# Moving the odd heads' keys on SyncE's queue in two parts, with ScalarE's key tiles ordered chunk by chunk

## The chip, the cores and the metric

The kernel runs on one core of one Trainium2 chip. A core has five engines that run side by side and wait for each other through semaphores: TensorE (matrix products), VectorE, ScalarE, GpSimd and SyncE (which here only issues transfers). The metric is the device time of one execution in microseconds. The profile is one further execution, recorded by the hardware profiler.

## What is computed

An attention with 32 heads that share one set of keys and values (head size 16, 2048 rows, width 512), and a gated MLP over the same rows, are mixed by a sigmoid gate.

```python
x = A_x                                             # 2048 x 512, bf16
g = sigmoid((x * gate_w).sum(-1, keepdims=True))
# A: 32 heads of 16, one key and one value head
q = (x @ wq).reshape(B, S, 32, 16).transpose(0, 2, 1, 3)
k, v = x @ wk, x @ wv
p = softmax(einsum('bhqd,bkd->bhqk', q, k) * 16 ** -0.5)
a = einsum('bhqk,bkd->bhqd', p, v).transpose(0, 2, 1, 3).reshape(B, S, 512) @ wo
# B: gelu, layer norm of one half, product with w_sp over the rows
z = gelu(x @ w_in)
z1, z2 = z[..., :688], layernorm(z[..., 688:])
b = (z1 * (w_sp @ z2 + b_sp)) @ w_out
out = g * a + (1 - g) * b
```

## The kernel before

**The attention in units.** The 2048 queries are cut into four chunks of 512, and the 32 heads into groups of eight. A unit is one query chunk with four heads, of even or of odd number in a group of eight; there are 32 units, even and odd in turn. The keys are cut into 16 tiles of 128 (tile kt belongs to chunk kt // 4). For one unit there are 64 blocks of scores: 16 tiles times four heads. Four heads use four row groups of 32 of TensorE at once.

**Keys for even and odd heads.** `KA` holds the transposed keys twice. `KA[:, 0, :]` has them in rows 0 to 15 of each row group of 32, for the even heads, and comes from VectorE's copy of a product in PSUM, one copy for each chunk (`k_ev`, line 355). `KA[:, 1, :]` has the same keys in rows 16 to 31, for the odd heads. [...]`k_shift` (line 359) issues four of them (one for each row group, all 2048 keys) on GpSimd's queue after chunk 3 has been copied.

**Two ways to an exponential.** ScalarE takes `exp` of two blocks at a time from PSUM into `P` (line 631). VectorE takes other blocks: a batch is one tile with four heads, and it makes a polynomial of the score by a scale and shift of two blocks at a time (`d_A`, line 655) and two squarings (`d_square`, line 667), into `X`; GpSimd can take pieces of 416 columns of the second squaring (line 674). A correction (`MC`, `CC`, made from `Kt` and the values) is added for the tiles that VectorE took in a unit. P and X are then multiplied with the values (`V1`) into one accumulating bank per unit.

**Which tile goes where.** `KL` lists the tiles: ScalarE takes a unit's tiles from its front, VectorE from its end, at most `NMAX` = 7 of them. `Kt` has keys replicated for the tiles that VectorE may take.

**The order is made by a planner.** A simulation in the kernel's Python code holds costs of each piece and due times (`T`), steps through TensorE, ScalarE and VectorE, and writes down each engine's instructions in the order in which it would start them. That order is fixed in the program; each engine follows its own list and waits on semaphores for the data. `T["K1"]` is the time from which the planner lets odd units begin. The first groups on TensorE are values and keys by chunk (`first`), then the correction, then queries, then the MLP's products (`g_z2`, `z1_mm`, `g_sp`).

**Fillers.** The planner counts TensorE's work of the last 3400 ns and puts in products that nobody reads (`ones`, `zeros`, in `keep_pick`) where it is under `KEEP`.

**Transfers.** At the start SyncE's queue issues the transposed loads of x, then the MLP's weights (`win`, `bspz`, `wo`, `wout`), then with `ld_wT(0)` four transposed loads of `w_sp` (line 302), each after the one before has landed. They are first used by `g_sp`.

```python
KL = (0, 1, 2, 4, 5, 8, 9, 12, 13, 6, 10, 14, 15, 11, 7, 3)
q = when(("Q", u // 2), ("K", 0, KL[un["hi"] // 4 - 1] // 4)) if u % 2 == 0 else when(("Q", u // 2), "K1")
rk = [("K", 0, kt // 4)] if par == 0 else [("K", 1, g)]
```

## Time and profile before

| | us |
|---|---|
| runs | 741.61, 739.71, 743.42, 744.69 |
| median of the runs | 742.52 |
| the profiled execution | 746.55 |
| its span | 744.7 |
| TensorE busy | 700.5 (94%) |
| VectorE busy | 713.5 (96%) |
| ScalarE busy | 719.0 (97%) |
| GpSimd busy | 303.2 (41%) |

The span is the time from the first to the last instruction of the profiled execution; 1.85 us of its time lie around it. A line of the profile's list of groups names the line of the code, the engine, the operation, what is written and read with its shape, how often, then the busy time and the mean of one in ns, and the idle time of the engine just before and what ended it. L312 and L313 are the helper that records every matmul, so these are told apart by their operands: `ps<-QA,KA` are scores, `ps<-P,V` and `ps<-X,V` the products with the values, `ps<-xT,wk_rep` keys, `ps<-wvg,xT` values and the gate, `ps<-ones,zeros` fillers. A timeline gives start and length of merged instructions of one kind, and in brackets the idle time before and its releaser.

### The profile page before, as it was taken

What the parts mean: (1) busy time and instruction counts of PE and PEld (TensorE: products, weight loads), DVE (VectorE), ACT (ScalarE), POOL (GpSimd) and SP (SyncE); (2) the same over time, 40 slices, a digit from 0 to 9 for tenths busy, and PEclk for the clock granted to TensorE, in tenths of its full rate; (3) what the DMA queues carried; (4) which work ended last, traced back from release to release, by engine and by line L of the source; (5) the groups of instructions that cost most, each with busy time, mean ns of one, the idle gap of its engine ahead of it and who ended that gap; (6) DMA issues with size and microseconds to landing.
All of it is one profiled execution on the core that took longest, in us unless ns stands there. A gap on an engine that the chain in (4) does not pass through costs nothing.

```text
span 744.7 us, 14117 instructions
## 1 busy us (share of the span) xinstructions
PE 700.5 (94%) x5529; PEld 192.4 (26%) x5529; DVE 713.5 (96%) x821; ACT 719.0 (97%) x781; POOL 303.2 (41%) x304
## 2 busy tenths in 40 slices
PE   8999999999899999999999999999999999999995
PEld 2222222223322223222222322222222222223221
DVE  7789999999999999999999999999999999999996
ACT  5789999999999999999999999999999999999994
POOL 4234334441434544444344343434454333334440
PEclk9779999999999999999999999999999999999998
DMA  9810000000000000600000050000005000000000
GB/s 193 191 34 1 1 1 1 1 1 1 1 1 1 1 1 2 116 13 15 1 1 1 2 121 15 8 1 1 1 2 113 16 15 1 1 1 1 1 1 33
DMA packets 49115, 17.06 MB, mean 23 GB/s; under 512 B 44146, under 2 KB 48978, under 8 KB 49043
## 3 DMA queue, kind: packets, MB, share of 16 engines
q1 hardware_dynamic: 45986, 15.02, 9.4%
q10 hardware_dynamic: 2928, 0.82, 0.6%
q8 instruction: 45, 0.74, 0.4%
q0 software_dynamic: 128, 0.26, 0.2%
q14 instruction: 28, 0.22, 0.1%
HBM read 3.25 MB, written 2.10 MB: 7 GB/s over the span
## 4 chain that ended last, share of the span: by engine, by line
ACT 57%; PE 22%; issue 17%; DVE 3%; DMA 1%; ACTq 0%
ACT P L631 55%; PE ps L313 14%; PE ps L312 7%; DVE X L655 1%; DMA xT<-in_A_x_dram 1%; ACT z L521 1%; DVE X L667 1%; ACT z L529 1%; DVE KA L355 0%; ACTq L161 0%; ACT L631 0%; ACT L529 0%; DVE outsb L1321 0%; DVE T L685 0%; DVE OT L700 0%
## 5 line engine op out<-in xcount | busy, mean ns | idle before, releaser
L631 ACT ACTIVATE P<-ps 128x1024 bf16<-128x1024 f32 x752 | 692.5, 1114 | 8.1 <-PE ps L313 7.8
L313 PE MATMUL ps<-QA,KA 32*128 32x512 bf16 x2048 | 320.2, 388 | 32.8 <-ACT P L631 27.3
L655 DVE TENSOR_SCALAR X<-ps 128x1024 f16<-128x1024 f32 x272 | 329.8, 1213 | 9.1 <-PE ps L313 7.9
L674 POOL TENSOR_TENSOR X<-X 128x416 bf16<-128x416 f16 x189 | 166.2, 879 | 348.8 <-DVE X L667 257.0
L667 DVE TENSOR_TENSOR X<-X 128x2048 f16<-128x2048 f16 (+3 forms) x272 | 291.0, 1076 | 2.0
L313 PEld LDWEIGHTS ps<-QA,KA 32*128 32x128 bf16 x2048 | 78.0, 91 | 322.3 <-ACT P L631 291.0
L313 PE MATMUL ps<-P,V 128*32 128x512 bf16 x1504 | 138.7, 389 | 0.0
L691 POOL TENSOR_TENSOR rc<-T,mone 128x16 f32<-128x16 f32 x31 | 94.7, 3056 | 54.4 <-DVE T L685 54.3
L312 PE MATMUL ps<-wT,z 128*128 128x512 bf16 x320 | 100.3, 385 | 0.0
L313 PE MATMUL ps<-X,V 128*32 128x512 bf16 x544 | 67.0, 388 | 0.2 <-DVE T L685 0.2
L313 PEld LDWEIGHTS ps<-P,V 128*32 128x32 bf16 x1504 | 28.6, 94 | 44.1 <-issue 43.2
L312 PEld LDWEIGHTS ps<-wT,z 128*128 128x128 bf16 x320 | 22.5, 97 | 47.6 <-issue 43.2
L312 PE MATMUL ps<-wout,z 128*128 128x512 bf16 x96 | 29.9, 385 | 0.7 <-DVE sq L613 0.4
L312 PE MATMUL ps<-win,xT 128*128 128x344 bf16 x128 | 29.6, 314 | 0.1
L685 DVE STREAM_TRANSPOSE T<-ps 128x512 f32<-128x512 f32 x32 | 22.7, 710 | 3.4 <-PE ps L313 3.3
L312 PE MATMUL ps<-ones 128*128 128x512 bf16 x64 | 22.3, 426 | 1.5 <-DVE ones L256 1.5
L312 PE MATMUL ps<-wo,OT 128*128 128x512 bf16 x64 | 21.4, 385 | 1.6 <-DVE OT L700 1.6
L697 POOL TENSOR_TENSOR Tn<-T,rcg 128x256 bf16<-128x256 f32 x31 | 21.3, 687 | 2.4
L312 PE MATMUL ps<-xT,wq 128*128 128x512 bf16 x64 | 20.5, 396 | 0.0
L312 PE MATMUL ps<-ones,zeros 128*128 128x512 bf16 x54 | 20.5, 406 | 0.0
L313 PEld LDWEIGHTS ps<-X,V 128*32 128x32 bf16 x544 | 15.6, 94 | 17.8 <-issue 15.7
L312 PE MATMUL ps<-xT,win 128*128 128x512 bf16 x80 | 18.3, 380 | 0.9 <-ACT z L521 0.7
(113 smaller groups left out, 293.6 us busy)
## 6 DMA issues: line engine op xcount, KB each, us to landing
out_dram<-outsb SPq DMA_DIRECT2D x14, 128.0 KB, 1.7
win<-in_B_w_in_dram SPq DMA_DIRECT2D x2, 688.0 KB, 6.0
wout<-in_B_w_out_dram SPq DMA_DIRECT2D x1, 640.0 KB, 9.2
wo<-in_A_wo_dram SPq DMA_DIRECT2D x1, 512.0 KB, 7.1
wq<-in_A_wq_dram ACTq DMA_DIRECT2D x1, 384.0 KB, 8.5
wT<-in_B_w_sp_dram SPq DMA_TRANSPOSE x16, 4.5
KA<-KA POOLq DMA_DIRECT2D x4, 64.0 KB, 3.5
out_dram<-outsb ACTq DMA_DIRECT2D x2, 128.0 KB, 3.3
```

The source lines that it names most:

```text
L312: return t.matmul(dst, lhsT, rhs, start=start, stop=stop)
L313: return t.matmul(dst, lhsT, rhs, start=start, stop=stop, tile_position=tp)
L521: op("act", lambda a: a.activation(z1[:, 1024 * i:1024 * i + 1024], bank(b, 1024), ACT.Gelu_apprx_tanh), r=[bkey(b), bkey(b + 1)], w=[("z1 ...
L529: op("act", lambda a: a.activation(z, z, ACT.Gelu_apprx_tanh), r=[("z2", st) for st in sts], w=[("z2", st) for st in sts], tag="gelu2")
L631: op("act", lambda a: a.activation(P[:, 512 * p:512 * (p + n)], ps[:, 512 * b0:512 * (b0 + n)], ACT.Exp), r=[bkey(b0 + i) for i in range(n ...
L655: op("dve", lambda v: v.tensor_scalar(X[:, m % NX, 1024 * h:1024 * h + 1024], bank(BD, 1024), PA, PB, ALU.mult, ALU.add), r=[bkey(BD), bke ...
L667: op(eng, lambda v: v.tensor_tensor(x if tag == "dU" else x.bitcast(B16), x, x, ALU.mult), r=ks, w=ks, tag=tag)
L674: op("pool", lambda g: g.tensor_tensor(x.bitcast(B16), x, x, ALU.mult), r=ks, w=ks, after=[pg.ops["dve"][-1]], tag="gW")
L685: o("dve", lambda v: v.transpose(T1[:], bank(BO)), r=[("bk", BO)], w=["T1"], tag="T1")
L691: o("pool", lambda g: g.tensor_tensor(rc[:].unsqueeze(2), lsum, mone[:].unsqueeze(2), ALU.pow), r=["T1", "mone"], w=["rc"], tag="rc")
L697: o(e, lambda v: v.tensor_tensor(tn, t1[:, :, 0:16], s_[:].unsqueeze(2).broadcast_to([128, 16, 16]), ALU.mult), r=["T1", k], w=[("Tn", pr, ...
```

## The change

The list of tiles is reordered so that ScalarE's front part has three tiles each of chunks 0, 1 and 2 and then the tiles of chunk 3, and VectorE's end is 3, 7, 11, 15, 14, 13, 12. The keys of the odd heads are moved in two parts, on SyncE's queue: keys 0 to 1535 after chunk 2 is copied, keys 1536 to 2047 after chunk 3 is. The first transposed loads of `w_sp` are issued behind the second part. Score products of odd units wait for the part that they read. The planner's `T["K1"]` is 5000 ns after chunk 3 in place of 4500. `Kt` gets the one tile of each of the chunks 0, 1, 2 and all four of chunk 3 that VectorE may now take.

```diff
-KL = (0, 1, 2, 4, 5, 8, 9, 12, 13, 6, 10, 14, 15, 11, 7, 3)
+KL = (0, 1, 2, 4, 5, 6, 8, 9, 10, 12, 13, 14, 15, 11, 7, 3)
...
-        ld_wT(0)
...
-        def k_shift():
+        def k_shift(z):
+
+            lo, hi = ((0, 1536), (1536, S))[z]
             for g in range(4):
-                dma("pool", lambda q, g=g: q.dma_start(KA[32 * g + 16:32 * g + 32, 1, :], KA[32 * g:32 * g + 16, 0, :]),
-                    r=[("K", 0, c) for c in range(4)] + ["KA1"], w=[("K", 1, g)], tag="Ksh")
+                dma("sp", lambda q, g=g: q.dma_start(KA[32 * g + 16:32 * g + 32, 1, lo:hi], KA[32 * g:32 * g + 16, 0, lo:hi]),
+                    r=[("K", 0, c) for c in (range(3) if z == 0 else (3,))] + ["KA1"], w=[("K", 1, g, z)], tag="Ksh")
...
+                if c == 2:
+                    k_shift(0)
                 if c == 3:
-                    k_shift()
-                    T["K1"] = t + 4500
+                    k_shift(1)
+                    ld_wT(0)
+                    T["K1"] = t + 5000
...
-                dve_q.append((330, lambda: op("dve", lambda v: v.tensor_copy(
-                    Kt[:, 2 * c:2 * c + 2, :].rearrange("p k (h d) -> p k h d", d=DH),
-                    KT0[:, 4 * c + 2:4 * c + 4, :].unsqueeze(2).broadcast_to([128, 2, 8, DH])), r=[("KT0", c)], w=[("Kt", c)], tag="Kt"), t, setT(("Kt", c))))
+                n, k0 = (1, 4 + c) if c < 3 else (4, 0)
+                dve_q.append((66 + 134 * n, lambda: op("dve", lambda v: v.tensor_copy(
+                    Kt[:, k0:k0 + n, :].rearrange("p k (h d) -> p k h d", d=DH),
+                    KT0[:, 4 * c + 4 - n:4 * c + 4, :].unsqueeze(2).broadcast_to([128, n, 8, DH])), r=[("KT0", c)], w=[("Kt", c)], tag="Kt"), t, setT(("Kt", c))))
...
-                        Kt[:, 2 * (kt // 4) + kt % 2, :] if h == 0 else ones[:, 0:128], V1[:, kt, :].unsqueeze(1).broadcast_to([128, NMAX - i, 32]),
+                        Kt[:, kt - 12 if kt > 11 else 4 + kt // 4, :] if h == 0 else ones[:, 0:128], V1[:, kt, :].unsqueeze(1).broadcast_to([128, NMAX - i, 32]),
...
-            rk = [("K", 0, kt // 4)] if par == 0 else [("K", 1, g)]
+            rk = [("K", 0, kt // 4)] if par == 0 else [("K", 1, g, kt // 12)]
```

## The prediction

> **What bounds the kernel now.** I read the page first, then ScalarE's timeline, then TensorE's, then a table of stretches. The page says which engine the end hangs on, and where the TensorE clock was not at full speed.

> ```profile
> span 744.7 us, 14117 instructions
> PEclk9779999999999999999999999999999999999998
> ACT 57%; PE 22%; issue 17%; DVE 3%; DMA 1%; ACTq 0%
> L631 ACT ACTIVATE P<-ps 128x1024 bf16<-128x1024 f32 x752 | 692.5, 1114 | 8.1 <-PE ps L313 7.8
> ```

> ScalarE's 752 exponentials are the longest part of the chain, and in the whole run they idle only 8.1 us. So the kernel is bound by ScalarE, and only those 8.1 us, the 10 us before the first exponential and the 10.7 us after the last are to be had. The second and third of the forty slices (18.6 to 55.9 us) have a granted clock of 0.7. ScalarE's timeline puts nearly all of the idle time there:

> ```profile
> 9.98 13.14 ACT L631 ACTIVATE P<-ps 128x1024 bf16<-128x1024 f32 x14 [0.49 <-PE ps L313]
> 24.56 3.77 ACT L631 ACTIVATE P<-ps 128x1024 bf16<-128x1024 f32 x4 [1.44 <-PE ps L313]
> 28.74 1.02 ACT L631 ACTIVATE P<-ps 128x1024 bf16<-128x1024 f32 x1 [0.31 <-PE ps L313]
> 46.02 1.02 ACT L631 ACTIVATE P<-ps 128x1024 bf16<-128x1024 f32 x1 [0.49 <-PE ps L313]
> 48.50 12.02 ACT L631 ACTIVATE P<-ps 128x1024 bf16<-128x1024 f32 x13 [0.16 <-PE ps L313]
> ```

> Fourteen exponentials run without a gap (0.939 us each), then one wait of 1.44 us, and from 28 to 48 us nearly every one waits for its score matmuls. TensorE's timeline shows what came first:

> ```profile
> 22.54 0.81 PE L312 MATMUL ps<-ones,zeros 128*128 128x512 bf16 x3
> 24.13 0.40 PE L313 MATMUL ps<-QA,KA 32*128 32x512 bf16 x4 [0.78 <-DVE KA L355]
> 24.46 0.57 PE L312 MATMUL ps<-wvg,xT 128*128 128x33 bf16 x16
> 24.87 0.59 PE L312 MATMUL ps<-ones,zeros 128*128 128x512 bf16 x2
> 25.64 0.39 PE L313 MATMUL ps<-QA,KA 32*128 32x512 bf16 x2 [0.17 <-ACT P L631]
> 26.55 0.61 PE L313 MATMUL ps<-QA,KA 32*128 32x512 bf16 x2 [0.53 <-ACT P L631]
> ```

> The score matmuls at 24.13 wait for VectorE's copy of the last key chunk. Tiles 0,1,2 of chunk 0, 4,5 and 8,9 are seven tiles of four heads, two (tile, head) blocks to an exponential: 14 of them, so the 15th is the first that needs chunk 3. The stall leaves a hole in TensorE's work, and the granted clock halves:

> ```profile
> 22.99:26.40 3.41, 2.08 (x26) 0.71 (x24) 3.38 (x7) 1.97 (x4) 2.33 (x5) 1.00 1.31 206
> 26.40:46.88 20.48, 20.33 (x130) 5.16 (x131) 13.23 (x29) 15.18 (x17) 2.48 (x4) 0.50 0.48 88
> 193.64:197.05 3.41, 2.11 (x10) 0.62 (x10) 3.21 (x9) 3.34 (x4) 0.53 (x1) 1.00 0.02 5
> ```

> (Columns: stretch, length, busy time of PE, PEld, DVE, ACT, POOL, then PEclk.) The low clock lasts 20.48 us, six times 3.41.

> [...] I count, from TensorE's timeline, each matmul as the share of the array it covers times columns/512. Window 22.99 to 26.40 has 4.5 by this count, the lowest; the lowest that kept the clock has 6.25 (at 691.9). Busy time doesn't separate them (2.08 fell, 2.11 at 193.64 held). [...] So keys moved by SyncE's queue stand behind the weights there. The trace has the neighbours:

> ```profile
> 18.24 0.43 SPq L296 DMA_DIRECT2D wout<-in_B_w_out_dram  x1
> 24.38 2.15 POOL L359 DMA_DIRECT2D KA<-KA  x4 [1.08 <-DVE KA L355]
> 28.55 11.98 SPq L302 DMA_TRANSPOSE wT<-in_B_w_sp_dram  x3
> ```

> **The change part by part.**

> *Order of the tiles.* With nine tiles in chunks 0 to 2, the first exponential that needs chunk 3 is the 19th, not the 15th. The score matmuls of exponential e go out when exponential e-2 ends, at 9.98 + 0.939(e-2): for e=19 at 25.94. When is chunk 3 copied? VectorE's order in the changed program has, after its first half batch of the second tile (15.97, as now), the chunk 2 copy. Its matmuls are now spread behind exponentials 8 and 9 (last one about 17.1), so the copy ends about 18.0 instead of 17.7. Then follow, in order, X L655 1.14, X L667 1.13, three copies of V 0.35, X L655 1.14, Kt 0.15, X L667 0.70; the next X L655 waits for its scores behind exponential 15 (22.2) and runs 22.95 to 24.1; then the chunk 3 copy, 0.60: ready at 24.7, 0.6 later than now (24.09). Needed 25.94: slack 1.2 us. The 1.44 us stall goes; if the slack were used up, ScalarE would pay only the excess. Late next is nothing nearer than this.

> *The low clock.* In the changed order TensorE's work from 22 to 27 us is: keys 0.5+2+0.5+1+0.5 to 24.1, eight P/X matmuls (2), scores 0.5, V (1.03), scores 0.5, one filler (1), scores, two fillers (2). With the times above, the poorest 3.41 us begin about 23.7 and count 6.0; starts before 23.5 and after 24.0 are over 6.5. That lies between the 4.5 that fell and the 6.25 that held, for some 0.3 us of starts out of 3.41; before, starts from 22.8 to 24 are under 6 and reach 4.5. So the clock most likely holds. Worth: from 23.12 to 48.50, 25.38 us, ScalarE did 18 exponentials and one small one; at 0.939 and 0.3 that is 17.2. Loss 8.2 us, of it 1.44 the stall, 6.7 the low clock. The cost of the low clock if it returns: the same 6.7 once per fall.

> *Does it reach the end?* After 48.50 ScalarE is busy 121.00 of 121.00 us (50 to 171) and 537.39 of 538 (196 to 734): what is gained at 48 is gained at 734. The two programs have the same 752 exponentials, 272 X L655, 544 X and 1504 P matmuls and corrections in all; three pieces of 416 columns go from GpSimd to VectorE (3 x 0.22 = 0.7 us, beside 10 us of idle VectorE after 196) and nine filler matmuls come in (9 x 0.22 = 2 us, beside some 20 us of idle TensorE there). Cost 0 while that idle holds, 2.7 at most without it. The Kt copies (three of 128 columns, one of 512, for four of 256 at 0.23) come to the same 0.9 us.

> *The key move.* GpSimd loses four issues (2.15 us), off the path. SyncE gets eight at 0.4 to 0.6 us. Part 1 waits for chunk 2 (18.0); SyncE reaches it at 18.67, so no wait, issued by 20.7. It lands when wout before it has: the last wout, issued 18.24, took 7.9 us, so about 26.3 to 26.6; the wT transpose now issued at 18.71 had landed at 28.55, an upper end. Who waits? The program's order names it: the first odd-unit score pair waits for part 1 alone, and stands right behind the scores of exponential 23 (29.7), so it is needed at 30.2. Slack 1.6 to 3.6. The second half of that pair's tile follows later. Part 2 is issued 24.7 to 26.7 and lands 3.3 to 3.8 us after (the four moves now), about 30.5; its tiles are needed past 40. Cost 0. Behind part 2 on SyncE's queue are the four wT transposes: they start at 26.7 instead of 18.71 and take at most the 21.8 us of now, landing by 53; first used at 212. Cost 0.

> *Sum.* The profiled execution took 746.55 us (span 744.7 and 1.85 around it): 746.55 - 8.2 = 738.3. Its own time is 4 us above the runs' median (742.52) and the fastest run (739.71) is 6.8 below it, nearly the 6.7 of the low clock: as if that run had not had it. Then the best to come is 739.71 - 1.44 = 738.3 too. I take **738.3**. If all runs fell as the profiled one did, it is 742.52 - 8.2 = 734.3.

> **The rivals.** *A, as worked out* (0.54): 738.3, own range 734.3 to 740.5. *B, one low window elsewhere* (0.16): the planner reorders the whole run, and a window under some 6 opens where none was; for it, the rolling count before also touches 5.0 at 481.8 and 5.5 at 111; against it, the clock held there. 738.3 + 6.7 = 745.0. *C, the timed runs mostly had no low clock* (0.08): then only the stall goes, 742.52 - 1.44 = 741.1. For it the fastest run; against it the median. *D, slower: the key move comes late* (0.12). TensorE takes its work in order, so at the odd-unit pair it stands still, ScalarE with it two exponentials later, and the hole lowers the clock. It decides from a landing of part 1 after 30.2; at 34, ScalarE loses 2 to 4 us and 6.7 more: 738.3 + 10 = 748. For it: 2.5 MB stand ahead in the same queue; against: 28.55. *E, two falls* (0.10): 751.7.

> **How the numbers follow.** About 0.5% (3.7 us) is what a measurement here tells from no change. Under 738.8 lies most of A, 0.46, and little else: faster 0.48. Same (738.8 to 746.2): the rest of A, B, C: 0.30. Slower: D, E: 0.22. Range 734.3 to 745.5 takes in A with both ends, C and B. Likeliest alone: 734.3 to 740.5.

> **What would show it.** Right: ScalarE's first run without a gap is 22 exponentials, to about 30.6, and goes on after it at 0.92 to 0.94; PEclk 1.00 from 23 to 50; the chunk 3 copy ends near 24.7; no TensorE wait on a DMA near 30. Wrong: a wait for KA before 26 (order), a PEclk of 0.5 anywhere (B, E), a wait for the key move (D). A time near 741 with a full clock would say C. ScalarE idle after 50 us would say that the new order cost something that I put at nothing.

## The result and the profile after

| | us |
|---|---|
| before, median of its runs | 742.43 (739.34 to 753.79) |
| changed, median of its runs | 736.79 (736.03 to 742.72) |
| ratio, 95% interval | 0.9924 (0.9908 to 0.994) |
| changed, the profiled execution | 737.94 |
| its span | 735.9 |

The ratios here and below leave out runs that lie more than 1.5% above the fastest of their kernel. The changed kernel is 0.6 to 0.9% faster. The profiled execution fell from 746.55 to 737.94, by 8.6 us; the prediction's sum was 8.2.

The page of the changed kernel answers to the lines shown of before:

```profile
span 735.9 us, 14140 instructions
...
PEclk9999999999999999999999999999999999999999
...
ACT 55%; issue 17%; PE 15%; DVE 11%; DMA 1%; SPq 0%; ACTq 0%
...
L636 ACT ACTIVATE P<-ps 128x1024 bf16<-128x1024 f32 x752 | 690.5, 1127 | 1.4 <-PE ps L312 1.3
```

No slice of the clock is under 9 tenths now. The same 752 exponentials have 1.4 us of idle time before them in the whole run (8.1 before) and 690.5 us of busy time (692.5 before). These two differences, 6.7 and 2.0, are nearly all of the 8.8 us by which the span is shorter. ScalarE's timeline shows where the idle time was:

```profile
10.64 2.86 ACT L636 ACTIVATE P<-ps 128x1024 bf16<-128x1024 f32 x3 [0.48 <-PE ps L312]
14.08 17.68 ACT L636 ACTIVATE P<-ps 128x1024 bf16<-128x1024 f32 x19 [0.59 <-PE ps L312]
31.65 0.22 ACT L448 ACTIVATE eg<-gs 128x16 f32<-128x16 f32 x1
31.76 9.37 ACT L636 ACTIVATE P<-ps 128x1024 bf16<-128x1024 f32 x10
41.33 19.38 ACT L636 ACTIVATE P<-ps 128x1024 bf16<-128x1024 f32 x21 [0.20 <-PE ps L312]
```

The wait of 1.44 us at the 15th exponential is gone; after the fourth there is none over 0.2 us. The wait of 0.59 us at the fourth comes from rows of x: TensorE waits 0.87 us for them, ahead of the scores of the fourth. Four other profiles of this order, below, have this wait too, with 0.29 to 0.59 us. The table of stretches, with the borders shown for before (columns: stretch, length, busy time of PE, PEld, DVE, ACT, POOL, then PEclk, DMA share, GB/s), has the full clock in both:

```profile
22.99:26.40 3.41, 3.41 (x30) 0.83 (x29) 3.30 (x6) 3.41 (x5) 0.96 (x2) 1.00 0.80 247
26.40:46.88 20.48, 19.19 (x185) 6.58 (x183) 17.63 (x36) 20.22 (x24) 5.12 (x4) 1.00 0.58 107
```

The span can be accounted for from the two timelines. Before, the first 32 exponentials take from 9.98 to 48.50 (38.52 us); changed, from 10.64 to 41.33 (30.69). That is 7.83 less. The other 720 take 685.33 before and 684.30 changed, 1.03 less. The first exponential starts 0.66 later, and what follows the last is 0.60 shorter (10.87 and 10.27). In sum -7.83 - 1.03 + 0.66 - 0.60 = -8.8, which is 735.9 - 744.7.

The profiled execution of before had a long stretch of low clock; not all its runs do. Every run is listed with its mean granted TensorE clock. One stretch of 3.41 us at 0.5 lowers the mean of a run by 1.7 / 740 = 0.0023, six lower it to 0.986. So a run with a single such stretch can still stand in the first row of the table (the profile of the kernel with the copy delayed, below, has one, and 0.995). The 193 runs of before that stand beside the experiments below, and the changed kernel's 59, sorted by this number:

| mean clock of the run | before: runs, mean us | changed: runs, mean us |
|---|---|---|
| 0.995 and over | 82, 739.77 | 47, 736.84 |
| 0.985 to 0.995 | 71, 743.86 | 9, 740.21 |
| under 0.985 | 40, 747.73 | 3, 744.95 |
| all | 193, 742.93 | 59, 737.76 |

Among the runs at 0.995 and over the changed kernel is about 3 us faster, and 20% of its runs are under 0.995, against 58%. With the times of before and the changed kernel's shares the mean would be 740.80: so of 5.2 us some 2.1 come from the rarer low clock and 3.0 from the rest.

### The profile page after: what moved, and what is told of

The parts are those of the page before. It is cut to its first block, busy times and chain, and to the rows that moved or that the text cites. A ratio compares the mean times of both kernels' runs of the same rounds, so it can differ in the third digit from the quotient of the medians.

```text
span 735.9 us, 14140 instructions
## 1 busy us (share of the span) xinstructions
PE 696.2 (95%) x5538; PEld 191.3 (26%) x5538; DVE 711.2 (97%) x821; ACT 716.9 (97%) x781; POOL 303.3 (41%) x297
## 4 chain that ended last, share of the span: by engine, by line
ACT 55%; issue 17%; PE 15%; DVE 11%; DMA 1%; SPq 0%; ACTq 0%
ACT P L636 55%; PE ps L312 9%; PE ps L311 6%; DVE X L660 5%; DVE X L672 3%; DMA xT<-in_A_x_dram 1%; DVE z L548 1%; DVE T L690 0%; DVE MC L471 0%; SPq L285 0%; DVE OT L705 0%; ACT L636 0%; ACTq L161 0%; ACT z L526 0%; DVE outsb L1326 0%
## 5 line engine op out<-in xcount | busy, mean ns | idle before, releaser
L636 ACT ACTIVATE P<-ps 128x1024 bf16<-128x1024 f32 x752 | 690.5, 1127 | 1.4 <-PE ps L312 1.3
L312 PE MATMUL ps<-QA,KA 32*128 32x512 bf16 x2048 | 315.0, 384 | 28.4 <-ACT P L636 24.2
L679 POOL TENSOR_TENSOR X<-X 128x416 bf16<-128x416 f16 x186 | 163.5, 879 | 333.5 <-DVE X L672 256.6
L312 PEld LDWEIGHTS ps<-QA,KA 32*128 32x128 bf16 x2048 | 77.5, 91 | 314.8 <-ACT P L636 293.8
L312 PE MATMUL ps<-P,V 128*32 128x512 bf16 x1504 | 136.4, 384 | 0.2 <-DVE T L690 0.2
L696 POOL TENSOR_TENSOR rc<-T,mone 128x16 f32<-128x16 f32 x31 | 98.3, 3171 | 60.3 <-DVE T L690 60.3
L312 PE MATMUL ps<-X,V 128*32 128x512 bf16 x544 | 65.9, 385 | 0.1
L312 PEld LDWEIGHTS ps<-P,V 128*32 128x32 bf16 x1504 | 28.6, 94 | 42.2 <-issue 41.1
L311 PE MATMUL ps<-wout,z 128*128 128x512 bf16 x96 | 30.2, 385 | 0.0
L311 PE MATMUL ps<-ones 128*128 128x512 bf16 x77 | 27.7, 425 | 1.8 <-DVE ones L256 1.4
L311 PE MATMUL ps<-wo,OT 128*128 128x512 bf16 x64 | 20.7, 384 | 1.1 <-DVE OT L705 1.1
L312 PEld LDWEIGHTS ps<-X,V 128*32 128x32 bf16 x544 | 15.6, 94 | 18.1 <-issue 15.9
L311 PE MATMUL ps<-ones,zeros 128*128 128x512 bf16 x50 | 17.6, 387 | 0.0
```

What stands on the lines that cost most here:

```text
L311: return t.matmul(dst, lhsT, rhs, start=start, stop=stop)
L312: return t.matmul(dst, lhsT, rhs, start=start, stop=stop, tile_position=tp)
L636: op("act", lambda a: a.activation(P[:, 512 * p:512 * (p + n)], ps[:, 512 * b0:512 * (b0 + n)], ACT.Exp), r=[bkey(b0 + i) for i in range(n ...
L679: op("pool", lambda g: g.tensor_tensor(x.bitcast(B16), x, x, ALU.mult), r=ks, w=ks, after=[pg.ops["dve"][-1]], tag="gW")
L696: o("pool", lambda g: g.tensor_tensor(rc[:].unsqueeze(2), lsum, mone[:].unsqueeze(2), ALU.pow), r=["T1", "mone"], w=["rc"], tag="rc")
```

## The experiments

Each kernel is compared with runs of before on the same chip. "Low" is the number of runs whose mean clock is under 0.995.

| kernel | median us | ratio, 95% interval | fastest us | low |
|---|---|---|---|---|
| order only (e_order_only) | 740.38 | 0.9979 (0.9954 to 1.0004) | 738.92 | 11 of 22 |
| key move only (e_move_only) | 742.61 | 1.0015 (0.9984 to 1.0045) | 739.07 | 9 of 14 |
| before, hole filled (e_before_fill) | 740.05 | 0.9977 (0.995 to 1.0004) | 738.59 | 8 of 22 |
| changed, copy delayed (e_after_late) | 739.98 | 0.9957 (0.9934 to 0.998) | 738.00 | 16 of 22 |
| order and 5000, old move (e_order_5000) | 737.00 | 0.9899 (0.9857 to 0.9941) | 735.96 | 0 of 6 |
| changed with 4500 (e_after_4500) | 740.67 | 0.9967 (0.9945 to 0.9988) | 738.57 | 11 of 22 |
| changed again (e_after_again) | 737.34 | 0.9941 (0.9914 to 0.9967) | 736.27 | 6 of 22 |
| changed, move behind w_sp (e_after_behind) | 749.20 | 1.0088 (1.0061 to 1.0115) | 746.84 | 18 of 18 |
| changed with 5500 (e_after_5500) | 739.47 | 0.9973 (0.9944 to 1.0001) | 736.74 | 13 of 22 |
| changed with 6000 (e_after_6000) | 741.94 | 1.0008 (0.9974 to 1.0041) | 738.98 | 7 of 14 |
| changed, copy delayed less (e_after_late_small) | 737.33 | 0.9927 (0.9902 to 0.9953) | 736.44 | 4 of 22 |
| changed, wait for x filled (e_after_start) | 737.43 | 0.9936 (0.9913 to 0.9959) | 736.66 | 6 of 22 |

### Which part brings it: order only, key move only

The order alone is the changed kernel with the keys moved as before, `T["K1"]` as before, and `w_sp` loaded early as before.

```diff
-                dma("sp", lambda q, g=g: q.dma_start(KA[32 * g + 16:32 * g + 32, 1, lo:hi], KA[32 * g:32 * g + 16, 0, lo:hi]),
+                dma("pool", lambda q, g=g: q.dma_start(KA[32 * g + 16:32 * g + 32, 1, :], KA[32 * g:32 * g + 16, 0, :]),
...
-                    T["K1"] = t + 5000
+                    T["K1"] = t + 4500
```

> The tile order and Kt changed, the key move left as before (one part, GpSimd's queue, after chunk 3). If the order makes the gain: ScalarE's first run without a gap reaches past its 18th exponential, clock 1.00 from 20 to 50 us, 736.5 to 738.5 us, ratio to before about 0.993. If the key move makes it: a wait of 1 us or more for KA's transfer near 30 us, or a low clock there, and 740 to 743 us. The odd pair of heads 0 and 1 stands behind exponential 23; the move can be issued only from about 25.5 to 27.7 us and takes 3.3 to 3.8 us more, so some wait at the edge is possible.

The median is 740.38, and the interval touches 1. The signs of the first half of the expectation are there, but not its time; the time is that of the second half, but TensorE waits for no key move in this profile. ScalarE's timeline and the group of exponentials in its profile:

```profile
9.40 3.01 ACT L632 ACTIVATE P<-ps 128x1024 bf16<-128x1024 f32 x3 [0.49 <-PE ps L313]
12.68 17.85 ACT L632 ACTIVATE P<-ps 128x1024 bf16<-128x1024 f32 x19 [0.27 <-PE ps L313]
...
30.52 129.68 ACT L632 ACTIVATE P<-ps 128x1024 bf16<-128x1024 f32 x141
```

```profile
L632 ACT ACTIVATE P<-ps 128x1024 bf16<-128x1024 f32 x754 | 692.8, 1123 | 1.2 <-PE ps L313 0.8
```

So the stall is gone, as predicted, and 141 exponentials follow without a gap. But there are 754 of them, two more than before: with this due time the planner gives ScalarE one batch of four blocks that VectorE has in the changed kernel. At 0.92 us each (692.8 / 754) that is 1.84 us on the engine that bounds the kernel, which takes back the 1.44 of the stall. From the first exponential to the end of the last it takes 717.00 us here, and 716.83 in the kernel before with the hole filled (below), where the stall is still there and the clock is full. The fastest runs fit this: 738.92 of 22 here, 738.35 of 67 in before.

The move alone keeps the old `KL` and `Kt` and takes all else of the change, the 5000 too.

```diff
-KL = (0, 1, 2, 4, 5, 6, 8, 9, 10, 12, 13, 14, 15, 11, 7, 3)
+KL = (0, 1, 2, 4, 5, 8, 9, 12, 13, 6, 10, 14, 15, 11, 7, 3)
```

> The key move in two parts on SyncE's queue, the old tile order. If the order makes the gain: the 15th exponential still waits for chunk 3 for about 1.4 us, the clock falls in a share of the runs as before, 740 to 744 us, ratio 0.998 to 1.002. If the key move makes the gain: 736.5 to 739 us.

No difference from before (1.0015), and ScalarE's timeline still has the stall:

```profile
26.74 3.77 ACT L635 ACTIVATE P<-ps 128x1024 bf16<-128x1024 f32 x4 [1.44 <-PE ps L312]
```

The table of stretches of this profile shows something that bears on the clock:

```profile
12.00:16.00 4.00, 3.64 (x17) 0.76 (x18) 3.56 (x5) 3.14 (x4) 0.00 (x0) 0.57 1.06 215
16.00:20.00 4.00, 4.00 (x19) 0.87 (x15) 2.52 (x4) 2.78 (x4) 0.88 (x1) 0.58 1.02 350
24.00:28.00 4.00, 3.05 (x32) 1.22 (x30) 3.96 (x5) 2.56 (x4) 0.88 (x1) 1.00 0.06 17
28.00:48.00 20.00, 17.72 (x172) 5.91 (x174) 18.49 (x38) 19.86 (x23) 5.53 (x5) 1.00 0.52 109
```

The stall is there, TensorE waits 0.78 us for the copy as in before, and yet the clock is full from 24 to 48 us. Its fall came earlier, from 12 to 20 us, and was (4 x 0.43 + 4 x 0.42) / 0.5 = 6.8 us long, two times 3.41. So the same hole is not always followed by a fall.

### The due time: order with 5000 and the old move, changed with 4500

The first kernel is the order-only one with `T["K1"] = t + 5000`. Its order on TensorE, VectorE and ScalarE is that of the changed kernel. The second is the changed kernel with one number put back.

```diff
-                    T["K1"] = t + 5000
+                    T["K1"] = t + 4500
```

> The key move as before (one part, GpSimd's queue) with the new tile order, and the planner's K1 at 5000 ns as in the changed kernel. TensorE, VectorE and ScalarE then have the changed kernel's order word for word; only the queue and the parts of the move differ. If the planner's order makes the gain: 752 exponentials, median 736.5 to 737.5 us, few low clocks (mean clock under 0.995 in about 1 run of 6). If the physical move counts (a late landing starves TensorE in some runs): median 738.5 us or more, low clocks in about half of the runs, as in the run with the order alone.

> The changed kernel with K1 at 4500 ns as before, nothing else. If the planner's order makes the gain: 754 exponentials as in the run with the order alone, floor 739 us (736.7 + 2 x 0.92 and a bit), low clocks in about half of the runs, median 739.5 to 741. If the physical move counts: a median of 737 to 738.6 (the two exponentials at most).

> The changed kernel itself on the same chip as the others, as their measure: median 736.5 to 737.5, mean clock under 0.995 in about 1 run of 6.

With 5000 and the old move 737.0, like the changed kernel on the same chip (737.34); with 4500 and the new move 740.67. So the number 5000 goes with the gain, and the new move does not. It takes both, though, the new order of the tiles and the 5000: the order with 4500 gives 740.38 and 740.67, the old order with 5000 (the move alone, above) 742.61. In the kernel with the old move TensorE waited 0.5 us for the keys of the odd heads, and ScalarE's timeline shows it:

```profile
34.22 6.52 ACT L632 ACTIVATE P<-ps 128x1024 bf16<-128x1024 f32 x7 [0.81 <-PE ps L313]
```

From first exponential to end of last this kernel took 715.67 us and the changed kernel, taken again, 714.96. The new move is worth up to 0.7 us in this pair of traces; the medians of 6 and 22 runs cannot show so little.

The kernel with 4500 has 754 exponentials again:

```profile
L636 ACT ACTIVATE P<-ps 128x1024 bf16<-128x1024 f32 x754 | 693.1, 1120 | 2.8 <-PE ps L312 2.4
```

### Is it the count, or the due time itself: 5500 and 6000

Two more values of the same number tell these apart, since the planner gives 752 exponentials with 5500 and 754 with 6000.

> The changed kernel with the due time of the odd units 5500 ns after chunk 3 in place of 5000. The planner writes another order from about the 30th exponential on, again with 752 exponentials on ScalarE (with 4500 it gives 754). Theory: what the due time is worth lies in the split that the planner happens to make; 752 exponentials then give 736 to 738, as 5000 did, and few runs with a mean clock under 0.995 (fewer than one in three). Rival 1: the due time as such decides, and 5000 is right because the odd keys have landed by then: 5500 costs some exponentials' wait at the first odd unit, 738 to 740. Rival 2: each new order is a draw of its own, with windows of low clock or without: then 5500 can lie anywhere from 736 to 741, apart from its count of exponentials.

> The changed kernel with the due time 6000 ns after chunk 3. The planner gives 754 exponentials, as with 4500. Theory (the split decides): two more exponentials of 0.92 us each on the engine that bounds, so 1.8 us over the kernel with 5500, and a fastest run near 738, not 736. Rival 1 (the due time as such decides): 5500 and 6000 stand together, or 6000 is a little slower than 5500 with no step in the fastest run. Rival 2 (each order is a draw): the share of low-clock runs differs from 5500's without regard to the count.

The fastest runs of the kernels without the stall follow the count: with 752, 736.74 (5500), 736.03 and 736.27 (5000, two sessions); with 754, 738.57 (4500) and 738.98 (6000). The medians do not: 5500 has the short count and yet 739.47, with 13 of 22 runs low. So each new order sets two things, and not the one with the other: the number of exponentials, worth some 2 us, and how often the clock falls. The theory held for the first (the busy time of the exponentials is 690.5 and 691.1 us with 752, and 692.8 to 693.8 with 754) and missed for the second, where the third expectation (each order is a draw of its own) held. These are four orders, so that the count isn't told from all else in which they differ. In the profiles of the 4500 and 6000 kernels the fall comes early, as with the move alone, after a wait of TensorE for x of 0.6 and 1.1 us. The table of stretches of the latter:

```profile
10.00:14.00 4.00, 2.16 (x24) 0.90 (x24) 3.93 (x9) 2.51 (x4) 0.00 (x0) 0.76 1.21 176
14.00:18.00 4.00, 4.00 (x20) 0.66 (x18) 2.26 (x4) 2.97 (x4) 0.55 (x1) 0.50 1.09 247
18.00:22.00 4.00, 4.00 (x17) 0.71 (x20) 1.81 (x3) 2.97 (x4) 0.33 (x1) 0.50 1.03 355
22.00:26.00 4.00, 3.55 (x44) 1.18 (x37) 3.96 (x8) 3.90 (x5) 0.88 (x1) 0.96 0.75 229
```

TensorE is busy 2.16 of the first 4 us; then the clock is at half for (4 x 0.24 + 8 x 0.5 + 4 x 0.04) / 0.5 = 10.2 us, three times 3.41, and ScalarE is busy 2.97 of each 4 us.

### Does the hole lower the clock: before with the hole filled

Before with six more products that nobody reads: four behind chunk 3's keys, two behind chunk 2's values. `load.pop()` keeps them out of the planner's count, so that the rest of the order stays. The stall stays; only the hole in TensorE's work is filled.

```diff
+        def fill(n):
+            for _ in range(n):
+                mm(bank(BO), zeros[:], ones[:], False, False, ["zeros", "ones"], [("bk", BO)], tag="keep0")
+                load.pop()
...
+            if (c, dt) == (3, 3):
+                fill(4)
...
+                if c == 2:
+                    fill(2)
```

> The kernel before with six more filler products, four behind the last product of key chunk 3 and two behind the values of chunk 2; nothing else moves. If the hole in TensorE's work halves the clock: no low clock near 26 us in any run, the stall of 1.4 us stays, and the median is 739 to 740 us with a small spread (before: 739.3 to 753.8). If the clock falls for another reason: median 742 to 743 and the same spread as before.

ScalarE's timeline and the table of stretches:

```profile
10.09 13.08 ACT L640 ACTIVATE P<-ps 128x1024 bf16<-128x1024 f32 x14 [0.49 <-PE ps L313]
24.64 3.77 ACT L640 ACTIVATE P<-ps 128x1024 bf16<-128x1024 f32 x4 [1.46 <-PE ps L313]
28.27 0.24 ACT L452 ACTIVATE eg<-gs 128x16 f32<-128x16 f32 x1
28.38 42.69 ACT L640 ACTIVATE P<-ps 128x1024 bf16<-128x1024 f32 x46
```

```profile
24.00:28.00 4.00, 3.51 (x52) 1.59 (x51) 3.25 (x10) 3.36 (x4) 2.15 (x4) 1.00 0.89 169
28.00:48.00 20.00, 18.14 (x168) 5.66 (x168) 19.18 (x32) 19.85 (x24) 6.41 (x6) 1.00 0.39 81
```

The stall is there, 1.46 us, and the clock holds: the 13 waits that follow in before are gone. The span is 737.3, 7.4 under the profiled execution of before. But the small spread of the expectation did not come (738.59 to 749.83). Over all runs the ratio, 0.9977, is not told from 1, and 8 of 22 runs are low, against 35 of 67 of before on this chip, which so few runs don't tell apart either. One execution with the fall against one without overstates what filling the hole is worth, and as the move alone has the full clock with the hole unfilled, this profile doesn't show that the filling held it. Where the clock fell in the 8 low runs is not known.

### How much slack the third key chunk has: the copy delayed

A memset of a part of the MLP's buffer, which is written later anyway, stands ahead of chunk 3's copy on VectorE. It only adds work.

```diff
         def k_ev(c, b):
+            if c == 3:
+                op("dve", lambda v: v.memset(z1[:, 4096:7168], 0.0), w=[("z1", 2), ("z1", 3)], tag="late")
```

> The changed kernel with a write of 128x3072 zeros on VectorE (to a buffer used later) ahead of the copy of key chunk 3, about 2.6 us, unknown to the planner. Slack of the 19th exponential in the changed kernel's trace: copy ends 25.9, needed 27.1, so 1.2 us. If the stall on chunk 3 is what costs: a ScalarE wait of about 1.4 us, TensorE starved around it, the clock falls in a large share of the runs; median 738 to 745 us. If the gain comes from elsewhere: 737 us, no change, since VectorE idles 2 us a little later.

```diff
+                op("dve", lambda v: v.memset(z1[:, 4096:5120], 0.0), w=[("z1", 2), ("z1", 3)], tag="late")
```

> The changed kernel with a memset of 128 x 1024 ahead of chunk 3's copy on VectorE, about 0.9 us, a third of the earlier experiment's. The slack measured in the changed kernel's profile is 1.18 us (copy done at 25.90, its scores due at 27.08). Theory (slack, then one to one): 0.9 is within it, ScalarE has no wait of 1 us or more near 27, median 736.5 to 738. Rival (any delay of VectorE there reaches ScalarE, since VectorE's own scores come later too): a wait of 0.5 to 1 us on ScalarE near 27 to 31, and 738 to 740 with low-clock runs at half.

The two memsets took 1.34 and 0.48 us, about half of what the expectations counted with. VectorE's timeline, first of the longer delay, then of the shorter:

```profile
24.42 1.34 DVE L355 MEMSET z<- 128x1536 uint32 x1 [0.27 <-issue]
25.67 0.63 DVE L356 CAST KA<-ps 128x512 bf16<-128x512 f32 x1
```

```profile
24.19 0.48 DVE L355 MEMSET z<- 128x512 uint32 x1
24.59 0.63 DVE L356 CAST KA<-ps 128x512 bf16<-128x512 f32 x1
```

With the shorter one ScalarE has 19 exponentials without a gap as in the changed kernel, and the median is the changed kernel's (737.33). With the longer one the stall is back, in ScalarE's timeline and in the clock:

```profile
27.29 1.94 ACT L638 ACTIVATE P<-ps 128x1024 bf16<-128x1024 f32 x2 [0.58 <-PE ps L312]
30.62 1.94 ACT L638 ACTIVATE P<-ps 128x1024 bf16<-128x1024 f32 x2 [1.40 <-PE ps L312]
```

```profile
27.50:31.00 3.50, 3.50 (x32) 0.96 (x32) 1.49 (x5) 2.10 (x3) 0.00 (x0) 0.51 0.27 64
```

and 16 of 22 runs are low, against 12 of the 59 of the changed kernel, with a median 2.6 us above that of the changed kernel taken again (739.98 and 737.34, on two chips). TensorE's timeline of the longer delay names who waited first:

```profile
26.36 0.57 PE L311 MATMUL ps<-wvg,xT 128*128 128x33 bf16 x16 [1.04 <-DVE KA L356]
```

It isn't the scores. The products for the next values write the bank that the copy reads, and in TensorE's order they stand ahead of the scores of the 19th exponential. In the changed kernel's profile the copy ends at 25.30 + 0.69 = 25.99, these products start at 26.48, the scores at 27.08. So the slack up to the first one who would wait is 0.5 us, not 1.1.

### The key move's place in the queue

The changed kernel with the first loads of `w_sp` ahead of the key move, where they stood before.

```diff
+        ld_wT(0)
...
                     k_shift(1)
-                    ld_wT(0)
```

> The changed kernel with the four transposed loads of w_sp ahead of the key move in SyncE's queue again. SyncE issues them one after the other landed until about 40 us (as before), so the keys land at 42 to 44 instead of about 30. If the odd pair behind exponential 23 is where a late move is paid: TensorE stands still from about 31.5 to 43, ScalarE loses about 10 us and the clock falls after it: 747 to 755 us. If there is other work to hide it: under 742.

This one is slower than before (ratio 1.0061 to 1.0115), and its fastest run, 746.84, lies above the median of before. SyncE's queue and ScalarE's timeline:

```profile
19.21 19.53 SPq L302 DMA_TRANSPOSE wT<-in_B_w_sp_dram  x4
38.79 5.03 SPq L361 DMA_DIRECT2D KA<-KA  x8
```

```profile
42.95 1.02 ACT L636 ACTIVATE P<-ps 128x1024 bf16<-128x1024 f32 x1 [10.77 <-PE ps L313]
45.30 15.01 ACT L636 ACTIVATE P<-ps 128x1024 bf16<-128x1024 f32 x16 [1.32 <-PE ps L313]
```

SyncE issues each of these loads after the last has landed: in before's trace the second to fourth are issued at 28.55, 33.14 and 38.04, and the one ahead of each landed at 28.54, 33.12 and 38.03. So here the moves are issued at 38.79, and TensorE waits 11.0 us for them. In the changed kernel the same two entries are

```profile
20.57 7.86 SPq L360 DMA_DIRECT2D KA<-KA  x8
28.47 16.59 SPq L302 DMA_TRANSPOSE wT<-in_B_w_sp_dram  x4
```

and no engine waits for a key move. The loads that are now late are first used at 189.4 (the prediction had 212).

### What is left: the wait for x filled

The changed kernel with three unread products ahead of chunk 1's keys, where TensorE waits for x. The rest of the order is the same.

```diff
         def k_mm(c, dt, b):
+            if (c, dt) == (1, 0):
+                for _ in range(3):
+                    mm(bank(BO), ones[:, 0:128], ones[:], True, True, ["ones"], [("bk", BO)], tag="keep0")
+                    load.pop()
```

> The changed kernel with three unread products of 128 x 512 on TensorE ahead of the first product of key chunk 1, where TensorE waits 0.87 us for x in the changed kernel's profile; the order of all else is the same. Theory: the low clocks that the changed kernel still shows (6 of 37 and 6 of 22 runs under 0.995) begin at this wait, so filling it leaves 0 to 3 of 22 and a median of 736.0 to 737.3, fastest run still 736. Rival 1: they begin elsewhere: 5 to 7 of 22 and a median like the changed kernel's, 736.8 to 737.4. Rival 2: where x comes early, the three products (0.66 us) stand ahead of scores that ScalarE waits for: 0.3 to 0.7 slower, 737.3 to 738.

Nothing moved: 6 of 22 low, 737.43. The rarer falls of the changed kernel are not shown to begin there. None of the five profiles with its order has a fall while the exponentials run (in the changed kernel's the clock is at half only from 733.9 us on, 3.8 behind the last product), so where they are stays open, and also why this order has fewer than those of 4500, 5500 and 6000. By the estimate of the last section, TensorE's work in the changed kernel's profile comes under 6.15 at two places only before its last products, in stretches of 3.41 us that begin from 9.9 to 12.1 us (the wait for x, filled here without effect) and near 656.7 us, where no run fills it. No kernel of the study beats the changed one beyond the intervals.

## Why the prediction was right

The median of 736.79 lies in the range (734.3 to 745.5), 1.5 us under the value of 738.3, and in the likeliest case, A. That the sum comes so near is in part luck. From the median of before the forecast is a gain of 4.2 us, that is 1.44 for the stall and 2.8 for the clock; in the means above the rarer low clock brought 2.1 and all else 3.0, so that one part was put too high and the other too low.

**The order of the tiles** did what the first step says. But for the wait for x at the fourth, the first 22 exponentials run without a gap. The copy was foreseen at 24.7 and needed at 25.94; in the changed kernel taken again, whose first exponential starts at 9.98 as in before, it ends at 24.61 + 0.69 = 25.30 and its scores start at 26.39. The slack to the scores came out at 1.1 where the prediction had 1.2. What the step missed is the group of values ahead of them, with 0.5.

**The low clock.** The cause is shown in one direction. With the stall brought back the clock falls right behind TensorE's wait and 16 of 22 runs are low, against 12 of 59 without it: the stall makes falls more frequent. That filling the hole prevents them is not shown (8 of 22 against 35 of 67), and of the two profiles with the stall of 1.44 us and the hole unfilled one, that of the move alone, has the full clock behind it. Why the one falls and the other doesn't is not shown; that a window of 3.41 us can start anywhere, on which the prediction's "0.3 us of starts out of 3.41" rests, was its author's estimate. What the traces show is the length: the delayed kernel's fall is one stretch of 3.5 us at 0.51, and in before it was six times 3.41. The prediction's 4.5 for the window that fell counts each product where it starts; with products shared out by their time it has 5.9 (the last section's estimate), much nearer to the lowest that kept the full clock in before, 6.27 at 333.6 us. In the changed kernel's profile no stretch of 3.41 us that begins from 20 to 32 us has under 6.8 by this count, where the prediction had 6.0 for the poorest.

**It reaches the end.** Right: after the first 32 exponentials the other 720 take 684.30 us, against 685.33 in before. Nothing was given back. (What follows the last exponential was 10.9 us in before, not 10.7.)

**The added work** at 0: nothing of it reached ScalarE. Of the 1.4 us idle before exponentials 1.27 stand in the lines shown (0.48, 0.59 and 0.20), so that 0.13 is left for all that follows. The profile gives no separate number for the nine products.

**The key move** at 0: right, and rival D is priced. Part 1 was to be issued by 20.7, and its first issue began at 20.57: in this execution the loads of x held the queue for 14.36 us (12.88 in before), and the issue of the last large load took 1.90 us (1.69). It landed 5.7 to 7.0 us after its issues, by 28.1, later than the 26.3 to 26.6 of the prediction and under its upper end of 28.55. It stood behind the weights on SyncE's queue, and in this trace they landed in the order of their issue: the last of the weights at 27.3, the four moves at 27.5, 27.7, 27.9 and 28.1. The same moves of 48 KB with none ahead of them, in the kernel with the move behind w_sp, landed in 2.6 us (median), here in 6.3. Rival D's mechanism exists, costs 11.9 us (749.20 against 737.34) when the keys are issued at 38.8, and was not met here.

**What was mis-sized: the base of the sum.** "Its own time is 4 us above the runs' median (742.52) and the fastest run (739.71) is 6.8 below it, nearly the 6.7 of the low clock: as if that run had not had it." That reading set the best to come at 738.3. With 193 runs, the runs of before at 0.999 or over lie at 738.35 to 739.5, so that 739.71 was probably not quite free of low clock (its own clock isn't on record); and the clock is no term of 6.7 that a kernel has or hasn't, but a share of runs with one fall, several, or none: 58% before, 20% after. The low end, 734.3, took the profiled execution's whole loss off the median of the runs; no run of any kernel here reached it.

**What was left out: the due time.** The prediction costs each edit but `T["K1"]`, from 4500 to 5000, has no term in it. With 4500 the change gives 740.67 and not 737.34, so 3.3 us, over half of the gain, hang on it: two exponentials by the planner's split, and falls of the clock in half of the runs. The sum came out right since it compared the two real programs, both with 752 exponentials, and not because the due time was reasoned about.

**What isn't settled.** Among the runs at 0.995 and over the kernels differ by 2.9 us. Of the profiles without a fall, before with the hole filled and the changed kernel taken again differ by 1.9 in the span: 1.1 in the idle time before exponentials (2.5 and 1.4; the stall of 1.46 is gone and the wait for x has come) and 0.7 in their busy time (691.2 and 690.5). The other 1.0 was not traced, and neither was why the exponentials are quicker by 0.7. The nine more products that nobody reads are a rival for the rarer falls that no run takes out.

## What to carry to other kernels

Where a planner writes the order, a due time changed by 500 ns is a change of the whole program (here 754 exponentials with 4500, 752 with 5000): count the instructions on the engine that bounds, and price that count, before a cause is sought in what the edit says it does. Where the clock falls in some runs only, one profiled execution shows the price of a fall and not how often it comes; compare the shares of runs and the fastest runs, each by itself. A slack ends at the first instruction in the queue that needs the same result or the same bank, which need not be the one that the change was made for: here 0.5 us to the values' products, and 1.1 to the scores.

## What was not expected of the hardware

The length of a fall varies: six times 3.41 us in before, three times in the kernel with 6000, two times in the move alone, one stretch of 3.5 in the delayed one. In the first TensorE was recorded busy 20.33 of 20.48 us and the clock still stayed at half.

The memsets were carried out as 128 x 1536 and 128 x 512 of a type twice as wide, in 1.34 and 0.48 us. And SyncE's issue of one move of keys took from 0.51 to 1.34 us, the longest for the last move of part 1.
